# Moving the loads of twelve MoE weights on the load queue, with a planner's tables set anew

## The chip, the core and the metric

The program runs on one core of one Trainium2 chip. The core has a matrix engine (TensorE, PE in the rows; its weight loads are listed apart as PEld), three engines for elementwise work (VectorE: DVE, ScalarE: ACT, GpSimd: POOL), a queue engine (SyncE: SP) from which nearly all DMA transfers are issued, and 16 DMA engines. Each engine runs its own instructions in program order and waits on semaphores for the others. The metric is the device time of one execution in microseconds (us).

## What is computed

```python
def _attn_ref(q, k, v):                      # q, k, v: (4, 8, 576, 64)
    ...
    q_d = q.reshape(B, H, Sd, factor, D).mean(axis=3)
    ...
    out_d = sm_attn(q_d, k_d, v_d)
    out_up = np.repeat(out_d, factor, axis=2)
    pos = np.arange(S)
    mask = np.abs(pos[:, None] - pos[None, :]) < factor
    scores = scale * np.matmul(q, k.transpose(0, 1, 3, 2))
    scores = np.where(mask, scores, -1000000000.0)
    ...
    out_local = np.matmul(attn, v)
    return (out_up + out_local).astype(np.float32)
...
def _moe_ref(x, w1, w2, w3, w_out):          # (2304, 512) -> 768 -> 512
    h = np.maximum(np.maximum(x @ w1, x @ w2), x @ w3)
    return (h @ w_out).astype(np.float32)
...
def _moe2_ref(x, w_in, w_out):               # (2304, 512) -> 2048 -> 512
    h = x @ w_in
    g = np.maximum(0.01 * h, h)
    return (g @ w_out).astype(np.float32)
```

The attention's output goes through the first of these layers, and that one's through the second. `factor` is 4: one attention over tokens pooled by four, one over a band of seven tokens.

## The kernel before

The 2304 tokens are eight **units** of 288 tokens, two to a batch. A unit goes through attention, then through the first MoE layer on PE: 18 steps `L{u}.{x}` (line 900: 12 matmuls into `ps_h`, for one of six column blocks m and one of three weights e, x = 3m + e) and the second product `Y{u}.{o}` (line 932, `ps_o`). Every float32 product is made of three products of halves, so each weight tile has to be split first: ACT makes two pieces (lines 390 and 391), DVE joins them (two instructions), ACT or DVE copies the high half (line 377) and POOL subtracts for the low half (`wA<-wy,wA` or `wO<-wy,wO`, some 1.27 us). There are 24 such tiles of 512 KB: `wA{m}_{e}` (18) and `wO{m}` (6), numbered 0 to 23 in the list `W1`. When all units are through, a second phase (lines 1121 and 1165) does the second MoE layer; it takes the time from about 424 us to the end.

**The start, written out by hand.** The attention of unit 0 and the first eight weight splits follow the string `ORDER` (line 45), one word for one step. For head pair n of batch 0, `a`, `s` and `p` load the query and key tile `sqk`, the value windows `sv` and the pooled values `dsrawv`; `C D E H I O o P Q R S` are the local attention (C scores on PE, E the exponentials `ple` on ACT, O transposes, P times values, Q the sum `x`, R and S its halves `xh` and `xl`); `A B F G J K M m N v` with `L` are the attention over pooled tokens (L pools the values on POOL, N gives `ps_up`, v copies it to `up`). `w5` loads weight tile 5; `x5 y5 z5 u5` are the four steps of its split. `M3+11` means: 11 matmuls on a blank tile ahead of M3, to keep TensorE working.

**Twelve of the 24 weight tiles share memory with the start.** The `late` buffers hold `ple`, `dsqke`, `dsrawv`, `dsvaT` and `plt` of batch 0, and become the tiles of weights 12 to 23 (`wA4_0` to `wA5_2`, `wO0` to `wO5`). `load_after` names for each buffer the step that uses it last: N0 for weight 12, P0 for 13, M2 for 14, L3 for 15, P1 for 16, O2 for 17, then M3, N2, O3, P2, N3, P3. Right behind that word, `load_w1` (line 381) puts the weight's load on SP's queue, where it waits until the buffer is free; what stands behind it on SP waits too.

**Everything after the start** is ordered by `Plan.order`, a planner that runs while the program is built: it simulates five engines with written-down durations, and on each engine begins the ready step with the earliest due time. Due times come from the pace of the units (`LEN`, planned us of each unit), moved for each kind of step by `SHIFT`; `SLACK` and `FLOOR` say how long before its due time, and before which planned time, a step may not begin; `LOADED` is when the planner takes SP to be free of the start's loads. Kinds that matter here: `co` is the split of the `wO` tiles, `c` that of the `wA` tiles, `ds1` the pooled attention of batch 1, `@` the second phase. Where the planner sees PE stand, it puts matmuls on `ident` (line 884, `keep`) into the gap.

Of the kernel before, what the change touches and what calls it, by code (L numbers as in the profile page):

```python
# [62 lines left out]
CONV = 8  # L63
# [1 line left out]

SHIFT = {"@": 13, "pv": 28.7, "ra": 42.5, "t": -60.1, "mu": 41.9, "c": 22.4, "ds3": -74.5, "ds2": -60.8, "pl3": -11.7, "pl1": 24.8, "co": 13.8, "pl2": 1.2, "ds1": 0.7}
SLACK = {"ds1": 107.4, "pv": 71.4, "c": 20, "mu": 155.4, "ds3": 65.3, "co": 9.5}
LEN = (56.9, 80.6, 30.2, 57, 39.6, 55.8, 30, 54.8)  # L70
GAP = 1.04
LOADED = 11.0
FLOOR = {}
BANKS = {"B": "early", "M": "at", "N": "mm", "O": "at", "C": "early"}
BOOST = {"at": 36.8, "early": 10.6}

# [1 line left out]
def kind(n):  # L78
    if n[0] == "@":
        return "@"  # L80
    if n[0] == "c" and int(n[2:]) >= NS:
        return "co"
    if n[0] == "t" or n[0] == "c":
        return n[0]
    if n[:2] in ("mu", "pm", "ps", "s1", "s2", "mk", "PV"):
        return {"mu": "mu", "PV": "ds" + n[2]}.get(n[:2], "pv")
    if n[0] in "rae":
        return "pv" if n[0] == "e" else "ra"
    if n[1].isdigit():
        return "pl" + n[1] if n[0] in "CDEHIOPQRSo" else "ds" + n[1] if n[0] in "ABFGJKMmNv" else ""  # L90
    return ""


class Plan:
# [22 lines left out]
    def order(self, due, shift, slack, gap):  # L117
# [27 lines left out]
        for n in due:  # L145
            due[n] += shift.get(kind(n), 0)
        begin = {n: max(due[n] - slack.get(kind(n), 1e9), st[n]["begin"], FLOOR.get(kind(n), -1e9)) for n in due}
        end, free, doing = {}, dict(dict.fromkeys(self.ENGINES, 0.0), SP=LOADED), {}
        left = {n: len(x["deps"]) for n, x in st.items()}
# [98 lines left out]
def local_global_attention_moe_kernel(  # L248
# [26 lines left out]
    W1 = [("A", m, e) for m in range(M1) for e in range(3)] + [("O", m) for m in range(M1)]  # L275
    w1_tag = {t: "w" + t[0] + "_".join(map(str, t[1:])) for t in W1}
    nl = len(W1) // 2
# [6 lines left out]
    load_after = {last[n]: nl + i for i, n in enumerate(sorted(last, key=lambda n: steps_.index(last[n])))}  # L284
# [65 lines left out]
    def scratch(first, kind, name):  # L350
        if first == 0:
            tag = "l3" if name == "wl3" else "b"
            return PS["0"].tile([128, 512], F32, tag=tag, bufs=6 if tag == "b" else 1, name=name)
        if kind == "mm":
            return mm_bank(name)
        return PS[kind].tile([128, 512], F32, tag=kind, name=name)
# [9 lines left out]
    def fill(t):  # L366
        for _ in range(fills[0]):
            T.matmul(out=t, lhsT=warm[:, :128], rhs=warm, start=True, stop=True)
        fills[0] = 0
# [9 lines left out]
    def load_weight(src, pool, name):  # L379
        w = pool.tile([128, 1024], I32, tag=name, bufs=1, name=name)  # L380
        nc.sync.dma_start(out=w, in_=src.bitcast(I32))
        return w, pool, name
# [41 lines left out]
    def conv_step(t):  # L424
        if t not in conv:
            conv[t] = split_steps(wr.pop(t), sup, P, 4, lambda: scratch("0" not in PS, "mm", "wl3"))
        r = next(conv[t])
        if r and t[0] == "A":
            wA[t[1:]] = r
        elif r:  # L430
            wO[t[1]] = r
        return r
# [99 lines left out]
    def pl_load(what, b, h, u=None):  # L532
        us = (0, 1) if b == 0 else (u,)
        if what == "a":
            t = pools[b].tile([128, 2 * S + 6], F32, tag="sqk", bufs=2 if b else 4, name="sqk")
            nc.sync.dma_start(out=t, in_=qk[b, h])
            if u in (None, 2 * b):
                dst[b, h, "q"], dst[b, h, "k"] = halves(t)
            for x in us:
                pl[x, h, "q"], pl[x, h, "k"] = t[:, :S], t[:, S:]  # L540
        elif what == "s":
            n, first = (1, u % 2) if b else (2, 0)
            t = pools[b].tile([KP, n, NBLK, 128], F32, tag="sv", bufs=1 if b else 4, name="sv")
            nc.sync.dma_start(
                out=t.rearrange("p u n d -> p (u n d)"),
                in_=vW[b, h][:, first * NBLK * 128 : (first + n) * NBLK * 128],
            )
            for k, x in enumerate(us):
                pl[x, h, "v"] = t[:KB, k]
        else:  # L550
            t = late_tile([QP, 2, 2, FAC, D], "dsrawv")
            nc.sync.dma_start(out=t.rearrange("p c h f d -> p (c h f d)"), in_=vP[0, h])
            dst[0, h, "vr"] = t

    def pl_pool_v(h):
        raw = dst.pop((0, h, "vr"))[:QC]
        dst[0, h, "vaT"] = late_tile([QC, 256 + 8 * QC], "dsvaT")
        v32 = dst[0, h, "vaT"][:, :256].rearrange("p (c h d) -> p c h d", c=2, h=2)
        P.tensor_tensor(out=raw[:, :, :, 0:2], in0=raw[:, :, :, 0:2], in1=raw[:, :, :, 2:4], op=ALU.add)
        P.tensor_tensor(out=v32, in0=raw[:, :, :, 0], in1=raw[:, :, :, 1], op=ALU.add)  # L560
        dst[0, h, "v"] = v32
# [310 lines left out]
    def mm_bank(name):  # L872
        banks_taken[0] += 1
        return PS["mm"].tile([128, 512], F32, tag="mm", name=name)
# [339 lines left out]
    with tc.manual_schedule(engines={ET.SP, ET.PE, ET.DVE, ET.Activation, ET.Pool}):  # L1214
# [4 lines left out]
        }  # L1219
        fills[0] = FILL0  # L1220
        fill(scratch(0, "", "warm_ps"))
        for w in ORDER.split():
            n = int(w[1])
            copy_on[0] = "DVE" if "'" in w else "ACT"
            fills[0] = int(w.split("+")[1]) if "+" in w else 0
            if w[0] == "w":
                load_w1(W1[n])
                if n == CONV - 1:
                    for t in W1[CONV:nl]:
                        load_w1(t)  # L1230
            elif w[0] in "aps":
                pl_load(w[0], 0, n)
            elif w[0] in "xyzu":
                conv_step(W1[n])
            elif w[0] == "L":
                pl_pool_v(n)
            else:
                steps[w[0]](0, n)
            if w[:2] in load_after:
                load_w1(W1[load_after[w[:2]]])  # L1240
        copy_on[0] = "ACT"
        fills[0] = 0
        PS.pop("0").release()
# [23 lines left out]
        for n in range(CONV, len(W1)):  # L1267
            f = lambda t=W1[n]: conv_step(t)
            go(f"cx{n}", "ACT", 1.3, f, begin=max(0.0, LOADED + 2.0 - 1.3 * (len(W1) - n)))
            go(f"cy{n}", "DVE", 1.4, f, [f"cx{n}"])  # L1270
# [135 lines left out]
        for u in range(NU):  # L1406
            base = sum(LEN[:u])
            pace = (LEN[u] - 10) / NS
            for x in range(NS):
# [56 lines left out]
        go("open4", "SP", 0.0, open_p2b, [f"st{NU - 1}.{o}" for o in range(4)] + [f"cu{n}" for n in range(CONV, len(W1))])  # L1466
        base2 = sum(LEN)

# [139 lines left out]
        for c in range(len(sups)):  # L1608
            t = 0.16 + 0.54 * sups[c][1] / SB
# [28 lines left out]
        done = 0.0  # L1638
        for n in pn.order(due, SHIFT, SLACK, GAP):
            x = pn.steps[n]  # L1640
# [86 lines left out]
```

## Time and profile before

| | us |
|---|---|
| median of 3 runs (lowest, highest) | 792.58 (792.56, 792.84) |
| the profiled execution's own time | 790.48 |
| its span, first to last instruction | 788.7 |
| PE busy; PEld busy | 767.2; 732.7 |
| DVE, ACT, POOL busy | 590.1, 453.2, 234.4 |
| mean granted TensorE clock | 0.991 of full |

The profile's times count from the first instruction. "Busy" adds the time in which an engine executes something; a PE that is busy may still be slower than it could be. The granted clock is 1.00 at 2.4 GHz and 0.50 at 1.2 GHz. The profiled execution is 2.1 us below the median of the runs, and its own time 1.8 us above its span.

### The profile page before, as it was taken

How to read it: one execution, taken by the hardware profiler on the slowest of the kernel's cores; microseconds unless marked ns; L12 is line 12 of the kernel's file. 1: busy time of each engine (PE TensorE's matmuls, PEld its weight loads, DVE VectorE, ACT ScalarE, POOL GpSimd, SP SyncE). 2: the span in 40 equal slices, each digit the busy share in tenths (PEclk: the TensorE clock that was granted, in tenths of full speed). 3: DMA queues.
4: the chain of work that ended last, by engine and by line, in shares of the span. 5: the costliest groups of instructions: out<-in, count | busy, mean ns of one | idle time of the engine just before them, and what ended most of it. 6: DMA issues, size and time to landing. Idle time of an engine off the chain costs nothing.

```text
span 788.7 us, 16482 instructions
## 1 busy us (share of the span) xinstructions
PE 767.2 (97%) x6182; PEld 732.7 (93%) x6182; DVE 590.1 (75%) x1076; ACT 453.2 (57%) x1534; POOL 234.4 (30%) x221
## 2 busy tenths in 40 slices
PE   8799899999999999999999999999999999999997
PEld 4488789989999999999999999999999999999996
DVE  6678855777987887848687886666688898878681
ACT  7588738875358842225266886776778443333330
POOL 5678779787878653100000000000000000000000
PEclk9979999999999999999999999999999999999999
DMA  9891144364343121223334568675798645453522
GB/s 304 265 406 43 57 161 136 119 204 165 89 129 98 46 66 48 72 73 100 99 108 138 200 245 305 238 261 213 238 345 295 211 127 168 129 148 109 151 72 63
DMA packets 53519, 127.08 MB, mean 161 GB/s; under 512 B 4992, under 2 KB 18176, under 8 KB 53440
## 3 DMA queue, kind: packets, MB, share of 16 engines
q1 hardware_dynamic: 48640, 121.06, 46.2%
q10 hardware_dynamic: 4800, 4.98, 1.8%
q8 instruction: 48, 0.79, 0.4%
q14 instruction: 31, 0.25, 0.1%
HBM read 90.37 MB, written 35.65 MB: 160 GB/s over the span
## 4 chain that ended last, share of the span: by engine, by line
PE 71%; POOL 5%; DVE 2%; issue 2%; ACT 1%; DMA 1%; ACTq 0%; DVEq 0%; POOLq 0%
PE acc L1165 22%; PE ps_h L900 19%; PE ps_y L1121 12%; PE ps_o L932 7%; PE ps_z L1121 6%; PE ps_x L1121 3%; POOL qkprod L240 2%; POOL ple L240 1%; DMA gd<-g 1%; PE ps_up L791 1%; POOL hl L240 1%; PE ps_x L831 0%; POOL sqk L240 0%; PE ps_aT L770 0%; DVE pvprod L240 0%
## 5 line engine op out<-in xcount | busy, mean ns | idle before, releaser
L900 PE MATMUL ps_h<-xh,wA 128*128 128x288 f32 x1152 | 199.9, 301 | 2.1 <-DVE x L240 1.3
L1165 PE MATMUL acc<-w,gs 128*128 128x256 f32 x1512 | 178.0, 280 | 0.0
L1165 PEld LDWEIGHTS acc<-w,gs 128*128 128x128 f32 x1512 | 177.7, 189 | 0.2 <-DVE ob L240 0.2
L900 PEld LDWEIGHTS ps_h<-xh,wA 128*128 128x128 f32 x1152 | 167.1, 188 | 7.6 <-issue 4.5
L1148 ACT ACTIVATE gs<-gr 128x1792 fp32r<-128x1792 f32 x36 | 61.0, 1703 | 90.5 <-DVE gr L240 55.9
L1121 PE MATMUL ps_y<-xop,w 128*128 128x288 f32 x768 | 110.1, 295 | 1.5 <-ACT u L1090 0.9
L900 PE MATMUL ps_h<-xl,wA 128*128 128x288 f32 x576 | 109.0, 296 | 0.0
L1121 PEld LDWEIGHTS ps_y<-xop,w 128*128 128x128 f32 x768 | 104.4, 189 | 2.3 <-ACT u L1090 1.1
L900 PEld LDWEIGHTS ps_h<-xl,wA 128*128 128x128 f32 x576 | 88.0, 189 | 0.0
L240 DVE TENSOR_TENSOR gs<-gr,gs 128x1792 fp32r<-128x1792 f32 x36 | 72.7, 2022 | 12.6 <-ACT gs L1148 12.3
L932 PE MATMUL ps_o<-hh,wO 128*128 128x288 f32 x384 | 79.7, 301 | 0.0
L240 POOL TENSOR_TENSOR qkprod<-lq,lk 128x1344 f32<-128x1344 f32 x24 | 73.7, 3078 | 7.6 <-issue 2.4
L470 ACT ACTIVATE qkprod<-qkprod 128x64 f32<-128x64 f32 x280 | 67.3, 245 | 9.5 <-POOL qkprod L240 8.3
L240 DVE TENSOR_TENSOR gr<-gr 128x256 f32<-128x256 f32 (+1 forms) x108 | 54.2, 511 | 19.4 <-DMA gr<-gd 17.8
L240 DVE TENSOR_TENSOR hm<-hm,ps_h 128x288 f32<-128x288 f32 x96 | 43.1, 449 | 27.4 <-PE ps_h L900 26.8
L932 PEld LDWEIGHTS ps_o<-hh,wO 128*128 128x128 f32 x384 | 61.1, 188 | 2.1 <-issue 1.4
L932 PE MATMUL ps_o<-hl,wO 128*128 128x288 f32 x192 | 56.7, 295 | 0.0
L1121 PE MATMUL ps_z<-xop,w 128*128 128x288 f32 x384 | 56.0, 294 | 0.0
L470 ACT ACTIVATION_READ_ACCUMULATOR qkprod<-qkprod 128x1 f32 x280 | 53.4, 191 | 0.0
L1121 PEld LDWEIGHTS ps_z<-xop,w 128*128 128x128 f32 x384 | 52.6, 189 | 0.0
L1102 ACT ACTIVATE g<-g 128x288 f32<-128x288 f32 x96 | 41.4, 442 | 17.5 <-DVE g L240 17.0
L240 DVE TENSOR_TENSOR g<-u,ps_z 128x288 f32<-128x288 f32 x64 | 28.5, 452 | 25.6 <-PE ps_z L1121 19.4
(142 smaller groups left out, 1217.7 us busy)
## 6 DMA issues: line engine op xcount, KB each, us to landing
gd<-g SPq DMA_DIRECT2D x32, 576.0 KB, 4.4
gr<-gd SPq DMA_DIRECT2D x32, 512.0 KB, 4.1
sqk<-in_qk_dram SPq DMA_DIRECT2D x20, 579.0 KB, 4.1
wA<-in_wa_dram SPq DMA_DIRECT2D x18, 512.0 KB, 9.8
wl<-in_w_in_dram SPq DMA_DIRECT2D x16, 512.0 KB, 3.5
wl<-in_w_out_dram SPq DMA_DIRECT2D x16, 512.0 KB, 6.0
wd<-w2y SPq DMA_DIRECT2D x8, 896.0 KB, 4.6
w2y<-wd SPq DMA_DIRECT2D x8, 896.0 KB, 6.4
```

The lines of the kernel that those rows point to most:

```text
L240: self.last = f(*args, **kwargs)
L470: A.activation(out=pr[:, r, j], in_=pr[:, r, j], func=AF.Copy, accum_out=sc[:, r, j : j + 1])
L791: T.matmul(out=ps[64 * hh : 64 * hh + 64, :SD], lhsT=dst[b, h, "v"][:, kc, hh], rhs=dst[b, h, "aT", kc][:, 2 * hh : 2 * hh + 2].rearrange( ...
L900: T.matmul(out=ps, lhsT=wA[m, e][wi][:, kk * 128 : kk * 128 + 128], rhs=xx[:, kk] if u < PEU else xx[:, :, kk, :], start=n == 0, stop=n == ...
L932: T.matmul(out=ps, lhsT=wO[m][wi][:, os_], rhs=xx[:, m], start=m == n == 0, stop=m == M1 - 1 and n == 2)
L1102: A.activation(out=g, in_=g if src is None else blk.pop((q, src)), func=AF.Prelu, alpha=0.01)
L1121: T.matmul(out=ps, lhsT=w[:, kk * 128 : kk * 128 + 128], rhs=xx, start=j in (0, 1, 3) and n == 0, stop=n == 5, skip_group_check=True,)
L1148: A.activation(out=ga[i][:, 0], in_=gr[i], func=AF.Copy)
L1165: T.matmul(out=acc[c, j][:, k * 256 : k * 256 + 256], lhsT=a[:, m : m + 128], rhs=w, start=p == 0 and k == 0 and n == 0, stop=p == NP - 1 ...
```

## The change

Two things are edited. In the loop over `ORDER`, a load into a late buffer is no longer issued behind the buffer's last step but kept in a list `waiting`; once the word `w7` has come, the loads of weights 8 to 11 and all that was kept are issued in order of the weight, and from then on each further one behind its step as before. And the planner's tables have other values (two lines of them stand here).

```diff
-LEN = (56.9, 80.6, 30.2, 57, 39.6, 55.8, 30, 54.8)
+LEN = (56.8, 80.6, 38.5, 58.8, 37.8, 55.7, 30.9, 55)
 ...
-LOADED = 11.0
-FLOOR = {}
+LOADED = 7.0
+FLOOR = {"ds1": 15.6}
 ...
+        waiting, loaded = [], False
         for w in ORDER.split():
             ...
             if w[0] == "w":
                 load_w1(W1[n])
                 if n == CONV - 1:
-                    for t in W1[CONV:nl]:
-                        load_w1(t)
+                    loaded = True
+                    waiting[:0] = W1[CONV:nl]
 ...
             if w[:2] in load_after:
-                load_w1(W1[load_after[w[:2]]])
+                waiting.append(W1[load_after[w[:2]]])
+            while loaded and waiting:
+                load_w1(waiting.pop(0))
```

On SP's queue, this stood behind the value windows of head pairs 0 and 1 (`sv`, the first two rows), some 11 us into the program; `dsrawv_427`, `sv_429`, `sv_435` (head pairs 2 and 3) and the tiles `wA2_0`, `wA1_2`, `wA2_1` (weights 6, 5 and 7) belong to the start, the `wA4` and `wA5` tiles are late ones:

```order
L544 DMA sv_316<-in_vW_dram 112x768
L544 DMA sv_410<-in_vW_dram 112x768
L381 DMA wA4_0_417<-in_wa_dram 128x1024
L552 DMA dsrawv_427<-in_vP_dram 80x1024
L544 DMA sv_429<-in_vW_dram 112x768
L544 DMA sv_435<-in_vW_dram 112x768
L381 DMA wA4_1_444<-in_wa_dram 128x1024
L381 DMA wA2_0_447<-in_wa_dram 128x1024
L381 DMA wA4_2_471<-in_wa_dram 128x1024
L381 DMA wA1_2_500<-in_wa_dram 128x1024
L381 DMA wA5_0_510<-in_wa_dram 128x1024
L381 DMA wA5_1_527<-in_wa_dram 128x1024
```

And now, at the same place of SP's queue:

```order
L544 DMA sv_316<-in_vW_dram 112x768
L544 DMA sv_410<-in_vW_dram 112x768
L552 DMA dsrawv_425<-in_vP_dram 80x1024
L544 DMA sv_427<-in_vW_dram 112x768
L544 DMA sv_433<-in_vW_dram 112x768
L381 DMA wA2_0_443<-in_wa_dram 128x1024
L381 DMA wA1_2_494<-in_wa_dram 128x1024
L381 DMA wA2_1_529<-in_wa_dram 128x1024
L381 DMA wA2_2_531<-in_wa_dram 128x1024
L381 DMA wA3_0_533<-in_wa_dram 128x1024
L381 DMA wA3_1_535<-in_wa_dram 128x1024
L381 DMA wA3_2_537<-in_wa_dram 128x1024
```

The late tiles now follow behind `wA3_2`, in the order of their use; which loads there are and how many has not changed.

On POOL, in the planned part, the low halves of the last weights of unit 0 (`hl` is a low half of the unit's first layer, `xl` one of unit 1's input, `ple` a step of unit 1's attention) stood in this order:

```order
L240 TENSOR_TENSOR wO0_1072<-wy_998,wO0_1072 128x512
L240 TENSOR_TENSOR wO1_1078<-wy_1023,wO1_1078 128x512
L240 TENSOR_TENSOR hl_770<-hm_1049,hh_769 128x288
L240 TENSOR_TENSOR ple_1088<-ple_1088,plsm_1089 96x612
L240 TENSOR_TENSOR wO2_1188<-wy_1045,wO2_1188 128x512
L240 TENSOR_TENSOR xl_1115<-x32_1116,xh_1114 128x288
L240 TENSOR_TENSOR hl_770<-hm_1171,hh_769 128x288
L240 TENSOR_TENSOR wO3_1259<-wy_1128,wO3_1259 128x512
L240 TENSOR_TENSOR wO4_1261<-wy_1152,wO4_1261 128x512
L240 TENSOR_TENSOR wA5_0_1269<-wy_1209,wA5_0_1269 128x512
L240 TENSOR_TENSOR wA5_1_1296<-wy_1244,wA5_1_1296 128x512
```

and now in this one:

```order
L240 TENSOR_TENSOR wA5_0_1065<-wy_973,wA5_0_1065 128x512
L240 TENSOR_TENSOR dsrawv_1002<-dsrawv_1002 72x4x128
L240 TENSOR_TENSOR dsv32_1103<-dsrawv_1002 72x256
L240 TENSOR_TENSOR wA5_1_1099<-wy_1043,wA5_1_1099 128x512
L240 TENSOR_TENSOR wA5_2_1135<-wy_1080,wA5_2_1135 128x512
L240 TENSOR_TENSOR hl_770<-hm_1038,hh_769 128x288
L240 TENSOR_TENSOR ple_1165<-ple_1165,plsm_1166 96x612
L240 TENSOR_TENSOR wO0_1202<-wy_1106,wO0_1202 128x512
L240 TENSOR_TENSOR hl_770<-hm_1163,hh_769 128x288
L240 TENSOR_TENSOR wO1_1239<-wy_1138,wO1_1239 128x512
L240 TENSOR_TENSOR wO2_1256<-wy_1196,wO2_1256 128x512
L240 TENSOR_TENSOR wO3_1275<-wy_1219,wO3_1275 128x512
```

The three `wA5` tiles, which the last three steps of `L0` read, now come ahead of all `wO` tiles, which `Y0` reads after them; ACT and DVE have the same order of splits. The start's steps on PE, ACT, DVE and POOL stand in the same order as before.

## Rows read from the trace of the kernel before

**Rows 1.** Stretches: PE, PEld, DVE, ACT, POOL busy (instructions), clock, DMA share, GB/s.

```profile
0.00:46.70 46.70, 37.96 (x288) 22.37 (x288) 31.45 (x78) 31.71 (x116) 29.91 (x36) 0.89 0.90 306
46.70:100.00 53.30, 49.02 (x421) 44.92 (x420) 45.54 (x103) 40.70 (x124) 42.75 (x49) 0.97 0.39 140
100.00:420.00 320.00, 318.93 (x2586) 305.28 (x2585) 241.32 (x464) 171.46 (x908) 161.74 (x138) 1.00 0.33 106
420.00:605.00 185.00, 183.48 (x1383) 182.70 (x1382) 133.15 (x254) 140.59 (x330) 0.00 (x0) 1.00 0.70 253
```

**Rows 2.** Timeline of SP's queue: start, length, line, transfer, count.

```profile
11.10 2.72 SPq L544 DMA_DIRECT2D sv<-in_vW_dram  x2
25.23 0.35 SPq L381 DMA_DIRECT2D wA<-in_wa_dram  x1
...
27.10 13.05 SPq L381 DMA_DIRECT2D wA<-in_wa_dram  x12
```

**Rows 3.** Waits of SP's queue to 52 us: for whom, total, times, longest.

```profile
SPq L381 <- PE ps_up L791: 11.3, 1, 11.3
```

**Rows 4.** Transfers issued from 13.3 to 13.9 us: KB, us from issue to landing.

```profile
sv<-in_vW_dram SPq DMA_DIRECT2D x1, 336.0 KB, 11.2
```

**Rows 5.** Stretches of two us, columns as in rows 1.

```profile
24.00:26.00 2.00, 2.00 (x30) 1.49 (x28) 1.23 (x6) 0.93 (x2) 1.73 (x2) 1.00 0.02 6
...
34.00:36.00 2.00, 2.00 (x6) 0.73 (x5) 0.00 (x0) 0.00 (x0) 2.00 (x2) 0.50 1.03 412
36.00:38.00 2.00, 1.42 (x8) 0.60 (x6) 0.00 (x0) 0.62 (x2) 1.54 (x2) 0.86 1.02 414
...
48.00:50.00 2.00, 2.00 (x12) 1.58 (x11) 1.86 (x4) 2.00 (x4) 1.50 (x2) 0.50 1.03 420
```

**Rows 6.** Timeline of ACT: start, length, operation, [idle before <-who ended it].

```profile
29.84 0.68 ACT L377 ACTIVATE dsvaT<-ps_aT 72x288 f32<-72x288 f32 x2
37.38 0.66 ACT L390 ACTIVATE wy<-wA 128x512 f32<-128x512 f32 x1 [6.86 <-DMA wA<-in_wa_dram]
...
40.40 0.67 ACT L390 ACTIVATE wy<-wA 128x512 f32<-128x512 f32 x1
```

**Rows 7.** Timeline of POOL at the pooled values of head pair 3.

```profile
31.11 1.26 POOL L240 TENSOR_TENSOR dsrawv<-dsrawv 72x512 f32<-72x512 f32 x1 [3.31 <-DMA dsrawv<-in_vP_dram]
```

**Rows 8.** Timeline of PE from the blank matmuls ahead of M3 to the end of L0.0.

```profile
32.93 4.24 PE L368 MATMUL ps_aT<-warm 128*128 128x512 bf16 x11 [1.46 <-DVE up L240]
37.00 0.41 PE L770 MATMUL ps_aT<-ident,dsqke 72*72 72x72 f32 x4
39.60 0.44 PE L770 MATMUL ps_aT<-ident,dsqke 72*72 72x72 f32 x4 [2.18 <-ACT ple L607]
40.57 1.23 PE L791 MATMUL ps_up<-dsvaT 72*64 72x144 f32 x8 [0.53 <-ACT ple L607]
...
46.73 0.61 PE L900 MATMUL ps_h<-xh,wA 128*128 128x288 f32 x1
...
51.08 0.29 PE L900 MATMUL ps_h<-xh,wA 128*128 128x288 f32 x1
```

**Rows 9.** Timeline of PE in unit 0 where it stood, and its first ps_o.

```profile
68.06 0.73 PE L884 MATMUL ps_h<-ident 128*128 128x224 bf16 x6 [1.05 <-DVE hm L240]
...
83.15 0.93 PE L884 MATMUL ps_h<-ident 128*128 128x224 bf16 x8 [1.11 <-DVE hm L240]
...
88.00 0.37 PE L900 MATMUL ps_h<-xh,wA 128*128 128x288 f32 x1 [1.33 <-DVE x L240]
...
89.31 0.53 PE L900 MATMUL ps_h<-xh,wA 128*128 128x288 f32 x2 [0.80 <-POOL wA L240]
...
95.58 0.43 PE L932 MATMUL ps_o<-hh,wO 128*128 128x288 f32 x2
```

**Rows 10.** Timeline of POOL at the low halves of wO3 and wO4, then wA5_2.

```profile
85.51 2.50 POOL L240 TENSOR_TENSOR wO<-wy,wO 128x512 fp32r<-128x512 f32 x2 [1.06 <-DVE wA L240]
...
92.41 1.27 POOL L240 TENSOR_TENSOR wA<-wy,wA 128x512 fp32r<-128x512 f32 x1
```

More of the change, by code (lines that the diff above doesn't have):

```diff
@@ L63 @@
 CONV = 8
-SHIFT = {"@": 13, "pv": 28.7, "ra": 42.5, "t": -60.1, "mu": 41.9, "c": 22.4, "ds3": -74.5, "ds2": -60.8, "pl3": -11.7, "pl1": 24.8, "co": 13.8, "pl2": 1.2, "ds1": 0.7}
-SLACK = {"ds1": 107.4, "pv": 71.4, "c": 20, "mu": 155.4, "ds3": 65.3, "co": 9.5}
-LEN = (56.9, 80.6, 30.2, 57, 39.6, 55.8, 30, 54.8)
+SHIFT = {"@": 8.7, "pv": 21.7, "ra": 7.2, "t": -44.8, "mu": 41.9, "c": 21.4, "ds3": -74.5, "ds2": -60.8, "pl3": -14.9, "pl1": 24.8, "co": 28.7, "pl2": 1.2, "ds1": -5.6}
+SLACK = {"ds1": 107.4, "c": 20, "mu": 155.4, "ds3": 65.3, "co": -32.2, "t": 17}
+LEN = (56.8, 80.6, 38.5, 58.8, 37.8, 55.7, 30.9, 55)
 GAP = 1.04
-LOADED = 11.0
-FLOOR = {}
+LOADED = 7.0
+FLOOR = {"ds1": 15.6}
 BANKS = {"B": "early", "M": "at", "N": "mm", "O": "at", "C": "early"}
```

## The prediction

> **What bounds the kernel now.** I read the stretches first, to see where PE stands still. From 100 us to the second phase PE is busy for 318.93 of 320 us, and in the next 185 us for all but 1.52; before 100 us it is not: 8.7 us of the first 46.7 and 4.3 of the next 53.3 are idle [rows 1]. So an edit can gain ahead of 100 us only, and what is gained there reaches the end if PE stays as full as it is behind it. Second, SP's queue: two `sv` loads, the last issued at about 13.5 us, then nothing until 25.23, and then twelve weight loads in a row [rows 2]; one wait of 11.3 us for N0's `ps_up` is the cause [rows 3]. The last `sv` landed 11.2 us after its issue, at 24.7 [rows 4], so the DMA engines ran dry: share 0.02 from 24 to 26 us, against 1.02 and 414 GB/s once the queue went on [rows 5]. Third, who stood for it: ACT for 6.86 us, until 37.38, for the tile of weight 6, with the exponentials E3 queued behind it [rows 6], and POOL for 3.31 us for the pooled values [rows 7]. PE's row of the start shows the end of the chain: eleven blank matmuls, M3's first half at 37.00, its second half only at 39.60, since it needs the bank that E3 reads, and `L0.0` at 46.73 [rows 8].
>
> **The change, part by part.**
>
> *The loads.* SP no longer stands behind N0. Of the six loads that matter, three are small (320, 336, 336 KB), then come the 512 KB of weights 6, 5 and 7. The first reuses a buffer whose last reader, O0, comes well ahead of N0 on PE, and all go out while the DMA engines still have work to 24.7. The small ones and weight 6 are 1.54 MB: at 414 GB/s [rows 5] 3.7 us, at the 306 GB/s of the whole start [rows 1] 5.0. Weight 6 lands between 28.4 and 29.7, weights 5 and 7 within 3.5 us more. ACT is free for it at 29.84 + 0.68 = 30.52 [rows 6]: the wait of 6.86 us goes. The pooled values land near 26, and POOL needs them only after its step before, so that wait goes as well. The twelve late loads each move behind seven others. With 19 tiles of 524 kB and 1.0 MB of small loads after 24.7, at 414 GB/s, the last lands at 24.7 + 26.5 = 51 us; the `wO` tiles were still being split at 85 us [rows 10]. No new wait there: cost 0. If that cover were gone, each missing tile would cost ACT its 1.3 us of transfer.
>
> *The chain that takes the wait's place.* ACT does weight 6 and E3 from 30.5 to 33.5 (they took 37.38 to 40.40 [rows 6]). But PE now stands on its own: the eleven blank matmuls wait for `up` until 32.93 and take 4.24 us at half clock to 37.0, as before, since nothing ahead of them has moved. So of ACT's 6.86 us PE gets only the 2.18 in front of M3's second half and the 0.53 in front of N2: M3 ends at 37.8 instead of 40.04. From N2 to `L0.0` before took 40.57 to 46.73, 6.16 us, all at clock 0.50 [rows 5, 8]. At full clock it is half of that, 3.1, or 3.7 if I leave some room between small steps: `L0.0` begins at 37.8 + 3.7 = 41.5 instead of 46.73, **5.2 us** sooner. `L0.0` itself, with its keep-alive matmuls, took 4.5 us at that clock (46.73 to 51.2); at full clock 2.4: its end is at 43.9, **7.3 us** sooner. ACT, DVE and POOL follow the first figure, PE the second. Through unit 0 the four are about equally full (PE 49.0, DVE 45.5, POOL 42.8, ACT 40.7 of 53.3 us [rows 1]), so I take **6.0**. The bounds: 2.7 (the two waits only, clock as before) and 7.3.
>
> *The clock.* It fell to 0.50 after the idle ahead of 32.93, came back during the blank matmuls (0.86 in 36 to 38), and fell again after PE had stood from 37.4 to 39.6 [rows 5, 8]. That second idle goes away, and dense small matmuls at 1.00 are in the trace too (24 to 26 us, 30 of them, PE busy throughout [rows 5]); so I take full clock. The Trainium skill (TensorE: Matmul & The Clock Gate, "The HAM clock gate") says that the low clock is the default and that sustained activity releases it. By that alone the work that began at 40.57 should have brought the full clock back well before 50; the row of 48 to 50 has 2.00 of 2.00 busy and still 0.50. The row decides: being busy is not enough here, and the low clock stays a rival.
>
> *The order in unit 0.* Four stands in 53 us: 1.05, 1.11, 1.33 and 0.80 [rows 9]. The last two are in front of `wA5` steps: `wA5_2`'s low half ends at 93.7 on POOL, and the first `ps_o` follows at 95.58, although `wO4` was ready at 88.0 [rows 9, 10]. With `wA5` ahead of `wO`, those 2.13 us go. In their place PE may wait for `wO4` in front of `ps_o`: it is now the last of the chain, with a step of E ahead of its copy on ACT. That costs nothing if `wO4` takes the place in time that `wA5_2` had. Between a gain of 4.3 (all four stands) and a loss of 4.3 (as many new ones) I take a gain of **1.5**, near the two that have a cause in the order.
>
> *The other tables.* They reorder steps from 100 us on. There PE has 1.07 us of idle to win [rows 1]; a poorer order costs, by its nearest row, what unit 0's stands are worth, 4.3. I take 0, since in the new order PE has the same steps, and DVE (241 of 320 us), ACT and POOL have room. Steps of the second phase become due 4.3 us sooner; PE hides them, and its own order there is a chain that does not change: 0, at most the 1.52 us of idle. The added Python costs the chip nothing.
>
> **Sum:** 6.0 + 1.5 = 7.5 us. The profiled execution, 790.48, would be 783.0; the median of the runs stands 2.1 above it, so 792.58 - 7.5 = **785.1 us**.
>
> **Rivals.**
>
> *The clock stays low* through 50 us, as it did before. Then `L0.0` gains 2.7 us only, and with the order 4.2: **788.4**. For it: the busy stretch at 0.50. Against it: the second idle is gone.
>
> *More is won.* The blank matmuls run at full clock as well (2.1 us), `L0.0` ends 7.3 sooner for all engines, and all four stands go: 2.1 + 7.3 + 4.3 = 13.7, at most **779**. Against it: everything ahead of 32.93 is as before. The Trainium skill (Perfetto Trace Analysis, "Identifying the Most-Contended Engine") calls the share of weight loads the better measure of PE's headroom; by PEld, 100 to 420 us has 14.7 us left instead of 1.07. But a stretch of small matmuls with PE full shows PEld at 1.49 of 2.00 [rows 5]: much of that is their shape, so it only adds to this rival's chance.
>
> *Given back.* In units 1 to 3 the new order makes PE wait for attention steps of DVE or POOL, by 4 to 7 us: about **791.5**, no change to be told. For it: DVE is three quarters full there, and all tables moved at once. Against it: PE's 1.07 us.
>
> *Slower.* The `wO` splits become the bound of unit 0. Before, PE took from 51.2 to 95.58 us for the other 17 steps, 44.4 with 4.3 of stands; from 43.9 on it has them behind it near 84, and cannot begin a `ps_o` before `wO4`'s low half. If ACT, with E and `hh` steps between, brings `wO4` later than 95.6 us, the time of the first `ps_o` before [rows 9], all is lost, and each us beyond it is one lost: at 97.5 **794.5**. By the forecast the first `ps_o` stands at 95.6 - 7.5 = 88, so it decides from a delay of 7.5 us. Against it: those splits start sooner by the 6 us.
>
> **How the numbers follow.** Forecast 0.53, clock low 0.18, more won 0.11, given back 0.10, slower 0.08. The forecast and its own spread cover 782.5 to 787.5. To leave out no more than 2 in 10, the range takes in the low clock and most of what lies below: **780.5 to 789.5**. About 0.2%, 1.6 us, is what runs of this kernel can tell from no change. Faster by more: 0.53 + 0.18 + 0.11 and a little of "given back", 0.85; within it 0.07; slower 0.08.
>
> **What would show it.** SP's queue has no gap between 17 and 30 us, and the DMA share no hole near 25; ACT begins weight 6 near 30.5 and E3 near 31.6; M3's second half follows its first at once; `L0.0` begins near 41.5, at clock 1.00; the first `ps_o` stands near 88; PE from 100 to 420 idles by no more than 2 us. Wrong, if `L0.0` starts later than 44, or if the lead at 100 us is not the lead at the end.

## The result, and the profile after

The changed kernel takes **783.61 us** (median of four runs, 782.19 to 786.43) against 792.57 for the kernel before beside it: a ratio of 0.9896 over all the runs (the two medians alone make 0.9887), 95% interval 0.9862 to 0.9930. The forecast was 785.1, with a range of 780.5 to 789.5.

The profiled execution of the changed kernel is the longest of its four runs (786.43, span 784.6), that of the kernel before (790.48) is shorter than all the runs of it beside these, so these two traces differ by 4.1 us where the medians differ by 9.0. Two more profiles of the changed kernel were taken: e11_again below (own time 780.97, the second shortest of its six runs) and e1_again (785.80, the longest of its six); the median of all sixteen runs is 782.3. The first profile and that of e11 ("the second") are read here, and e1's stands beside them where it says something else. The span splits into six stages on PE: up to the first matmul of `L0.0`; from there to the first `ps_o` of unit 0; to unit 1's first `ps_h`; units 1 to 3 up to unit 3's first `ps_o`; up to unit 7's first `ps_o`; to the end.

| us | to `L0.0` | unit 0 | to unit 1 | units 1 to 3 | to unit 7 | rest | span |
|---|---|---|---|---|---|---|---|
| before | 46.7 | 48.9 | 15.3 | 138.3 | 165.9 | 373.6 | 788.7 |
| after, first profile | 41.2 | 43.5 | 15.7 | 144.5 | 166.6 | 373.1 | 784.6 |
| after, second profile (e11) | 38.8 | 43.2 | 15.7 | 141.8 | 166.4 | 373.3 | 779.2 |
| after, e1 | 40.5 | 44.0 | 15.7 | 143.3 | 166.2 | 374.1 | 784.0 |

The gain lies in the start (5.5 to 8.0 us) and in unit 0 (4.8 to 5.6); 3.5 to 6.2 us of it are lost again in units 1 to 3. The rows for that, beginning with the stretches of the first profile (columns as in [rows 1]):

```profile
0.00:46.70 46.70, 38.66 (x331) 24.27 (x332) 36.04 (x85) 35.23 (x123) 33.37 (x42) 1.00 0.99 328
46.70:100.00 53.30, 51.66 (x453) 47.50 (x452) 42.94 (x100) 39.38 (x119) 41.97 (x46) 1.00 0.31 104
100.00:420.00 320.00, 317.38 (x2543) 304.27 (x2542) 242.15 (x468) 170.06 (x908) 159.19 (x135) 0.99 0.35 110
```

PE's idle from 46.7 to 100 us is 1.64 instead of 4.28 us, the clock of the start is 1.00 instead of 0.89, and the DMA share of the start 0.99 instead of 0.90. From 100 to 420 us PE idles 2.62 us, where it had 1.07 [rows 1]. SP's queue has lost its hole (timeline as in [rows 2]):

```profile
11.78 2.79 SPq L544 DMA_DIRECT2D sv<-in_vW_dram  x2
17.31 0.31 SPq L552 DMA_DIRECT2D dsrawv<-in_vP_dram  x1
17.67 1.62 SPq L544 DMA_DIRECT2D sv<-in_vW_dram  x2
19.95 18.82 SPq L381 DMA_DIRECT2D wA<-in_wa_dram  x13
```

The thirteen `wA` loads now go out from 19.95 us on; in [rows 2] one went out at 25.23, behind the wait, and twelve from 27.10. In the stretch 24 to 26 us, empty before (0.02 [rows 5]), the DMA engines are full (but at 213 GB/s, half of what they move later), and two later stretches that stood at clock 0.86 and 0.50 are at 1.00:

```profile
24.00:26.00 2.00, 1.22 (x14) 0.71 (x14) 1.97 (x4) 0.51 (x1) 0.72 (x1) 1.00 1.05 213
36.00:38.00 2.00, 2.00 (x17) 1.21 (x17) 1.48 (x6) 2.00 (x8) 1.58 (x2) 1.00 1.04 414
48.00:50.00 2.00, 2.00 (x17) 2.00 (x17) 1.78 (x5) 2.00 (x7) 1.82 (x4) 1.00 1.04 424
```

ACT's wait of 6.86 us for weight 6 [rows 6] is 0.66 in the first profile, nothing in the second and 2.19 in e1 (one row of each, in this order):

```profile
33.55 0.67 ACT L390 ACTIVATE wy<-wA 128x512 f32<-128x512 f32 x1 [0.66 <-DMA wA<-in_wa_dram]
...
30.46 0.68 ACT L390 ACTIVATE wy<-wA 128x512 f32<-128x512 f32 x1
...
33.24 0.68 ACT L390 ACTIVATE wy<-wA 128x512 f32<-128x512 f32 x1 [2.19 <-DMA wA<-in_wa_dram]
```

PE in the start, first profile (columns as in [rows 8]):

```profile
34.91 2.55 PE L368 MATMUL ps_aT<-warm 128*128 128x512 bf16 x11 [1.50 <-DVE up L240]
37.30 0.67 PE L770 MATMUL ps_aT<-ident,dsqke 72*72 72x72 f32 x8
...
41.20 0.40 PE L900 MATMUL ps_h<-xh,wA 128*128 128x288 f32 x1
...
44.81 0.29 PE L900 MATMUL ps_h<-xh,wA 128*128 128x288 f32 x1
```

The eleven blank matmuls run at full clock, 2.55 us instead of 4.24 [rows 8]; M3's two halves follow each other without the 2.18 us between. This profile reached the blank matmuls 2.0 us later than the kernel before. Some 0.7 us of that stood already at 14 us, ahead of the first load that moved. The rest goes back to DVE, which stood 2.12 us, until 23.63, for a `sqk` load of the start: issued at 9.29 us, it took 14.3 us to land, against 11.9 in the kernel before (issued at 8.82). Whether the moved loads, which share the DMA engines with it from 17 us on, slowed it is not shown. The second profile does not have that lag:

```profile
32.46 2.55 PE L368 MATMUL ps_aT<-warm 128*128 128x512 bf16 x11 [0.94 <-DVE up L240]
34.85 0.67 PE L770 MATMUL ps_aT<-ident,dsqke 72*72 72x72 f32 x8
...
38.75 0.40 PE L900 MATMUL ps_h<-xh,wA 128*128 128x288 f32 x1
...
58.91 0.54 PE L884 MATMUL ps_h<-ident 128*128 128x224 bf16 x4 [0.71 <-DVE hm L240]
...
70.83 0.54 PE L884 MATMUL ps_h<-ident 128*128 128x224 bf16 x4 [0.88 <-DVE hm L240]
...
82.00 0.53 PE L932 MATMUL ps_o<-hh,wO 128*128 128x288 f32 x2
```

The rows at 58.91 and 70.83 are what is left of unit 0's stands: 0.71 and 0.88 us instead of 1.05, 1.11, 1.33 and 0.80 [rows 9]; the two in front of the `wA5` steps are gone, and the first `ps_o` is at 82.0 (84.65 in the first profile) instead of 95.58.

### The profile page after: what moved, and what is told of

It is laid out like the page before. It is cut to its first block, busy times and chain, and to the rows that moved or that the text cites. A ratio compares the mean times of both kernels' runs of the same rounds, so it can differ in the third digit from the quotient of the medians.

```text
span 784.6 us, 16494 instructions
## 1 busy us (share of the span) xinstructions
PE 765.3 (98%) x6186; PEld 732.6 (93%) x6186; DVE 590.8 (75%) x1078; ACT 453.3 (58%) x1532; POOL 234.5 (30%) x221
## 4 chain that ended last, share of the span: by engine, by line
PE 83%; POOL 5%; DVE 4%; DMA 4%; issue 2%; ACT 1%; ACTq 0%; DVEq 0%; SPq 0%; POOLq 0%
PE ps_h L900 25%; PE acc L1165 23%; PE ps_y L1121 13%; PE ps_o L932 8%; PE ps_z L1121 6%; PE ps_x L1121 3%; DMA sqk<-in_qk_dram 2%; POOL qkprod L240 2%; PE ps_sc L722 1%; DVE wl L240 1%; PE ps_up L791 1%; DMA dsrawv<-in_vP_dram 1%; DVE wy L240 1%; POOL wA L240 1%; PE ps_lo L652 1%
## 5 line engine op out<-in xcount | busy, mean ns | idle before, releaser
L900 PE MATMUL ps_h<-xh,wA 128*128 128x288 f32 x1152 | 200.5, 302 | 0.0
L900 PEld LDWEIGHTS ps_h<-xh,wA 128*128 128x128 f32 x1152 | 168.1, 190 | 5.2 <-issue 3.1
L900 PE MATMUL ps_h<-xl,wA 128*128 128x288 f32 x576 | 110.2, 298 | 0.4 <-POOL xl L240 0.2
L900 PEld LDWEIGHTS ps_h<-xl,wA 128*128 128x128 f32 x576 | 88.6, 190 | 1.1 <-POOL xl L240 1.1
L470 ACT ACTIVATION_READ_ACCUMULATOR qkprod<-qkprod 128x1 f32 x280 | 55.3, 198 | 0.0
```

The lines of the kernel that those rows point to most:

```text
L470: A.activation(out=pr[:, r, j], in_=pr[:, r, j], func=AF.Copy, accum_out=sc[:, r, j : j + 1])
L900: T.matmul(out=ps, lhsT=wA[m, e][wi][:, kk * 128 : kk * 128 + 128], rhs=xx[:, kk] if u < PEU else xx[:, :, kk, :], start=n == 0, stop=n == ...
```

## The experiments

All twelve stand here; "before" is the kernel before, run beside each on the same chip. A ratio is taken over all the runs and can differ a little from the quotient of the medians.

| | median, us (runs) | before | ratio, 95% interval |
|---|---|---|---|
| e1_again, changed kernel | 782.23 (6) | 792.38 | 0.9873, 0.9843 to 0.9902 |
| e2_loads_only | 783.63 (6) | 792.38 | 0.9890, 0.9864 to 0.9916 |
| e3_tables_only | 789.83 (12) | 792.38 | 0.9974, 0.9950 to 0.9999 |
| e4_keep_on | 782.49 (6) | 792.38 | 0.9870, 0.9845 to 0.9896 |
| e5_no_blanks | 784.75 (12) | 791.14 | 0.9935, 0.9908 to 0.9963 |
| e6_w6_late | 790.31 (12) | 791.14 | 0.9977, 0.9949 to 1.0006 |
| e7_wO_early | 790.87 (12) | 791.14 | 0.9985, 0.9960 to 1.0010 |
| e8_before_fill | 790.83 (12) | 791.86 | 0.9978, 0.9958 to 0.9997 |
| e9_fewer_blanks | 786.01 (6) | 791.86 | 0.9912, 0.9887 to 0.9937 |
| e10_w6_late_look | 788.94 (1) | 791.86 | |
| e11_again, changed kernel | 781.86 (6) | 790.95 | 0.9881, 0.9853 to 0.9909 |
| e12_loads_only | 785.50 (6) | 790.95 | 0.9925, 0.9897 to 0.9952 |

**The two parts apart.** The changed kernel again (e1, e11), the moved loads with the tables of before (e2, e12), and the new tables with the loads where they were (e3).

```diff
 e2, e12: the changed kernel with
+SHIFT, SLACK, LEN, LOADED, FLOOR of the kernel before
 e3: the changed kernel with
-        waiting, loaded = [], False
 ...
+                load_w1(W1[load_after[w[:2]]])
```

> The changed kernel once more. Its four runs lay between 782.19 and 786.43 us, those of before mostly within 0.3 us. Theory A (PE's clock falls in only some executions, near 207 us, where PE stood for 1.5 us in the profiled one): runs spread again over 4 us, median 782 to 785, and a profile whose clock does not fall there is 2 to 4 us shorter than the first. Theory B (the first profile is how it always runs): spread under 1 us, about 785.

> Only the loads are moved; the planner's tables are those of before. If the lead comes from the loads (my theory): L0.0 begins at 41 to 42 us, and the time is 785 to 787.5, since the stands in front of the wA5 steps (1.33 and 0.80 us) come back. If the tables carry it (rival): 789 to 793. The first ps_o should stand at 88.5 to 91.

> Only the tables are changed; the loads are issued as before. My theory: SP stands to 25 us as before and L0.0 begins at 46.5 to 47; the new order of the splits alone gives 1 to 3 us in unit 0, and the planner now expects the loads sooner than they come: 789 to 793. Rival (the tables carry the gain): 784 to 787.

> The changed kernel once more, beside the moved loads alone, to settle two things: whether its time is that of its second look (782.2) or nearer to that with 8 blank matmuls (786.0), and what the tables are worth on top of the loads. Theory A (the tables' lead of unit 0 is mostly given back in units 1 to 3): 782 to 784.5, and 0.5 to 2.5 us below the moved loads alone. Theory B (the lead is kept in most executions, the profiled ones fell into the low clock at the seam of units 2 and 3): 3 us or more below the moved loads alone.

> The moved loads with the planner's tables of before, once more, on the same chip as the changed kernel. Theory A (most of unit 0's lead given back): 784 to 786, 0.5 to 2.5 us above the changed kernel beside it. Theory B: 3 us or more above it.

The loads alone take 8.8 us off in the first set of runs and 5.4 in the second, the tables alone 2.6 (0.1 to 4.0 by the interval). Over both sets the changed kernel has a median of 782.0 us (12 runs) and the loads alone 784.6 (12 runs), so on top of the loads the tables are worth some 2.6 us as well (the means differ by 2.5, 95% interval 1 to 4): 1.4 in one set and 3.6 in the other. Neither theory of the last pair is shown outright; the two sets lie on either side of the line drawn between them.

The stages tell more. Moved loads with old tables: 38.8, 49.5, 15.3, 138.4, 165.9, 375.7 us (e2) and 40.2, 51.3, 15.3, 138.4, 165.9, 374.6 (e12). New tables with old loads: 45.5, 44.1, 15.7, 144.7, 166.1, 373.2 (e3). So the start follows the loads, and unit 0 and units 1 to 3 follow the tables.

Part of the difference in unit 0 is the clock. The old tables keep the stands in front of the `wA5` steps (1.33 and 0.81 us in e12), and in the profiles of e12, e2 and e8 (below) the clock fell at them, for some 7, 3 and 7 us, as it did not in the kernel before. In no profile with the new tables is there such a stretch in unit 0 behind 50 us. A row of e12, then one of e8:

```profile
84.00:88.00 4.00, 4.00 (x19) 3.96 (x18) 1.92 (x6) 2.13 (x7) 4.00 (x4) 0.50 0.00 0
...
88.00:92.00 4.00, 3.62 (x15) 3.62 (x16) 3.47 (x8) 3.59 (x13) 4.00 (x5) 0.50 0.00 0
```

Why unit 0 wins what units 1 to 3 lose shows in the attention's matmuls of unit 0, grouped by line (busy, mean ns of one, idle before); first with the old tables, e12:

```profile
L579 PE MATMUL ps_ls<-sqk 64*96 64x102 f32 x60 | 3.9, 260 | 0.0
L631 PE MATMUL ps_lt<-ident,ple 96*102 96x96 f32 x24 | 3.0, 267 | 0.0
...
L652 PE MATMUL ps_lo<-plt,sv 102*64 102x96 f32 x38 | 2.4, 254 | 0.0
```

and with the new ones, e11:

```profile
L579 PE MATMUL ps_ls<-sqk 64*96 64x102 f32 x48 | 3.1, 260 | 0.0
L631 PE MATMUL ps_lt<-ident,ple 96*102 96x96 f32 x18 | 2.0, 245 | 0.0
L652 PE MATMUL ps_lo<-plt,sv 102*64 102x96 f32 x26 | 1.7, 254 | 0.0
```

Twelve matmuls fewer of L579, six of L631 and twelve of L652 (and two of L571): one head pair of unit 1's local attention is no longer done in unit 0. In a timeline such a group takes 0.77, 0.70, 0.72 and 0.42 us, 2.6 together. In units 1 to 3 of the same two traces its L652 and L631 come back, with eight of L722 that stood ahead of unit 1 before, where its L579 and L571 are now:

```profile
L652 PE MATMUL ps_lo<-plt,sv 102*64 102x96 f32 x84 | 5.0, 254 | 0.0
...
L631 PE MATMUL ps_lt<-ident,ple 96*102 96x96 f32 x42 | 4.6, 245 | 0.0
...
L722 PE MATMUL ps_sc<-dsqk 64*72 64x144 f32 x40 | 3.6, 297 | 0.0
```

```profile
L652 PE MATMUL ps_lo<-plt,sv 102*64 102x96 f32 x96 | 5.7, 255 | 0.0
...
L631 PE MATMUL ps_lt<-ident,ple 96*102 96x96 f32 x48 | 5.3, 245 | 0.0
...
L722 PE MATMUL ps_sc<-dsqk 64*72 64x144 f32 x48 | 4.6, 298 | 1.0 <-ACT aT L377 1.0
```

(first e12, then e11). By these rows that is 0.7 + 0.7 + 1.0 = 2.4 us of work moved in, and the last row has a stand of 1.0 us on top. About half of unit 0's gain over the kernel before was work put off.

**The seam of units 2 and 3.** In the new order PE stands twice there, for ACT. In e11 nothing more came of it; in the first profile of the changed kernel the clock fell behind it (PE timeline of e11, then of the changed kernel):

```profile
203.91 0.44 PE L770 MATMUL ps_aT<-ident,dse 72*72 72x72 f32 x4 [0.54 <-ACT up L377]
205.35 1.01 PE L722 MATMUL ps_sc<-dsqk 64*72 64x144 f32 x8 [1.00 <-ACT aT L377]
206.28 0.79 PE L900 MATMUL ps_h<-xh,wA 128*128 128x288 f32 x4
```

```profile
206.50 0.44 PE L770 MATMUL ps_aT<-ident,dse 72*72 72x72 f32 x4 [0.54 <-ACT up L377]
207.94 1.53 PE L722 MATMUL ps_sc<-dsqk 64*72 64x144 f32 x8 [0.99 <-ACT aT L377]
209.40 1.33 PE L900 MATMUL ps_h<-xh,wA 128*128 128x288 f32 x4
```

The stands are equal to 0.01 us, yet in the second block eight L722 take 1.53 instead of 1.01 us and four L900 1.33 instead of 0.79. The stretch behind them, changed kernel (clock 0.50) and e11 (1.00):

```profile
208.00:212.00 4.00, 4.00 (x19) 3.63 (x20) 3.86 (x6) 0.18 (x1) 2.58 (x5) 0.50 0.33 107
```

```profile
208.00:212.00 4.00, 4.00 (x32) 4.00 (x32) 3.86 (x7) 1.96 (x9) 3.33 (x2) 1.00 0.48 148
```

This is the 2.7 us by which the two profiles differ in units 1 to 3 (144.5 and 141.8). In e1 the same stands were followed by some 3 us at 0.50, and units 1 to 3 took 143.3. Of the eight profiles with these stands (e3, e5, e6, e9 and e10 have them too) the clock fell in five and stayed at 1.00 in three (e6, e10, e11). The Trainium skill (TensorE: Matmul & The Clock Gate, "The HAM clock gate") says of the start of a kernel that how much work runs at the low clock differs from run to run. These traces show the same in the middle of one, behind stands of 1.5 us in all. Filling the seam was one experiment: the planner's matmuls on `ident`, allowed up to 150 us of the planned time, allowed up to 400, which adds 19 of them there.

```diff
-KEEP_TO = 150.0
+KEEP_TO = 400.0
```

> The changed kernel with the planner's fill-in matmuls allowed up to 400 us of planned time instead of 150: 19 more of them, all at the seam of units 2 and 3, where PE stood in the first profile and its clock fell to 0.50 for 7 us. Theory A (the low clock there costs 3 to 4 us): clock 1.00 from 205 to 216 us, unit 3 begins 2 to 4 us sooner against the same profile's first ps_o of unit 2, median 780.5 to 782.5 and a smaller spread. Rival: the 19 matmuls only take their 2 us, no change.

Its profile shows no stretch below 1.00 up to the last few us, and 142.2 us in units 1 to 3, but its median, 782.49, is not below the 782.23 of e1, nor is the median of its mean clocks (0.998) above that of e1 (0.999). Its profile alone cannot show that the matmuls kept the clock, since e6, e10 and e11 kept it without them; and if they did, it was worth less than these runs can tell.

**Weight 6.** In the changed kernel, the loads of weights 8 to 11 ahead of those of weights 6, 5 and 7: no gap on the queue, only other tiles first.

```diff
+                if n == 6:
+                    for t in W1[CONV:nl]:
+                        load_w1(t)
                 load_w1(W1[n])
                 if n == CONV - 1:
                     loaded = True
-                    waiting[:0] = W1[CONV:nl]
```

> The changed kernel with the loads of weights 8 to 11 put ahead of the load of weight 6: the same transfers without a gap on the queue, but weight 6 lands later by four tiles of 524 kB, 5.1 us at the 414 GB/s of the trace before. Theory A (the gain of the loads is the landing of weight 6, which holds ACT, the exponentials E3 and M3): ACT waits some 5 us for it, M3's second half stands 2 to 3 us behind its first, the clock falls to 0.50, L0.0 begins near 45 to 46, and the time is 4 to 6 us above the changed kernel: 786 to 788. Theory B (the gain is that the DMA engines no longer run dry, whichever tile comes first): the time is within 1.5 us of the changed kernel, 781 to 783.7.

> A second look at the kernel with the loads of weights 8 to 11 ahead of weight 6, whose profiled execution was one of its fast ones. Theory A (its slow runs are the clock): a run near 788 to 791 shows more than the 8 us at clock 0.50 of the first look, mean clock near 0.991. Theory B: as many us at 0.50 as in the first look, and longer waits of ACT for weight 6.

The order of those tiles costs 8.3 us against the changed kernel's 782.0 (7.9 by the ratios to the kernel before on each chip, 0.9977 and 0.9877), more than the 4 to 6 expected, and leaves 0.8 us of the gain, which these runs cannot tell from none. The three small loads go out early here as in the changed kernel, so they are not what won the time. Rows of e10, ACT and then PE:

```profile
36.68 0.66 ACT L390 ACTIVATE wy<-wA 128x512 f32<-128x512 f32 x1 [6.19 <-DMA wA<-in_wa_dram]
```

```profile
35.14 0.41 PE L770 MATMUL ps_aT<-ident,dsqke 72*72 72x72 f32 x4
38.90 0.69 PE L770 MATMUL ps_aT<-ident,dsqke 72*72 72x72 f32 x4 [3.35 <-ACT ple L607]
...
46.03 0.61 PE L900 MATMUL ps_h<-xh,wA 128*128 128x288 f32 x1
```

This is the start of the kernel before again, with full DMA engines: a wait of 6.19 us on ACT (6.86 in [rows 6]), M3 in two halves, and `L0.0` at 46.03 (46.73 in [rows 8]). Weights 5 and 7 came later too, but ACT goes on to them without a wait, at 39.71 and 43.33. In e6, whose profiled run (787.45, span 785.7) lies 2.9 us below its median, M3's halves were 1.42 us apart and `L0.0` began at 43.2. Theory B, that full DMA engines were the gain, falls. That the price is above 5.1 us is only partly explained: by its windows e10 ran some 10 us at clock 0.50 and e6 some 7, and the mean clocks of the twelve runs, median 0.9915, lie below those of both profiles (0.993 and 0.994), so that most runs had more of it.

**The clock of the start.** Two edits at the word M3 of the changed kernel, and one in the kernel before.

```diff
 e5: the changed kernel      e9: the changed kernel      e8: the kernel before
-M3+11                      -M3+11                      -M3+11
+M3+0                       +M3+8                       +M3+24
```

> The changed kernel without the eleven blank matmuls ahead of M3. Theory A (the clock is a term of its own in the gain: the blank matmuls now end at full clock, and M3 to L0.0 follow at full clock): PE stands some 3 us ahead of M3 (the exponentials E3 still end near 36.7 us), the granted clock falls to 0.50 as it did in the kernel before, the small steps from M3 to L0.0 take some 6 us instead of 3.5, L0.0 begins near 43.5 to 44.5 instead of 38.6 to 41.2, and the time is 2 to 3 us above the changed kernel: 784 to 785.5. Theory B (the clock decides nothing here, the chain of ACT and DVE sets the pace): L0.0 begins within 1 us of the changed kernel and the time is within 1 us of it, 781.5 to 783.

> The changed kernel with 8 blank matmuls ahead of M3 instead of 11. In the profile of the changed kernel the eleven end at 37.3 us, and E3 at 36.7, so the last three stand in M3's way. Theory A (eight are enough for the clock): M3 0.6 us sooner, the mean clock as in the changed kernel, the time 0 to 0.7 us below it. Theory B (the eleven hold the clock up): the mean clock of the runs falls below 0.995 and the time rises by 1 to 3 us, towards that without any blank matmul.

> The kernel before with 24 blank matmuls ahead of M3 instead of 11; the loads stay where they were. The blanks cover most of the stretch from 32.9 to 39.6 us in which PE stood for the exponentials E3, so the granted clock should come back during them and stay. Theory A (half of the gain of the change is the clock, which its moved loads keep up): M3's second half is still held by weight 6 and E3 near 39.6, but M3 to the end of L0.0 runs at 1.00; the mean clock of the runs rises from some 0.992 to 0.996 or more and the time falls by 3 to 5 us, to 787 to 789, against 792 for the kernel before on this chip. Theory B (the clock in the start is a companion, the chain of ACT decides): the time is within 1.5 us of the kernel before.

Without blank matmuls (e5) the clock falls and the time is 2.8 us above the changed kernel's 782.0 (4.6 by the ratios on each chip). PE's rows, and a stretch:

```profile
34.48 0.94 PE L770 MATMUL ps_aT<-ident,dsqke 72*72 72x72 f32 x8 [2.15 <-POOL dsqke L240]
...
41.64 0.61 PE L900 MATMUL ps_h<-xh,wA 128*128 128x288 f32 x1
```

```profile
36.00:40.00 4.00, 4.00 (x30) 2.83 (x30) 3.40 (x9) 4.00 (x9) 4.00 (x4) 0.50 1.02 414
```

From M3 to `L0.0` it is 7.16 us at the low clock; the changed kernel has 3.90 (37.30 to 41.20, and 34.85 to 38.75). That is as theory A had it, though `L0.0` began at 41.64, sooner than its 43.5 to 44.5; this profile (789.09, the second longest of the twelve) has the low clock at the seam as well. But e8 speaks against the wider reading that the clock by itself is half of the gain: the kernel before with 24 blank matmuls was expected at 787 to 789 and is at 790.83, 1.0 us below the kernel before (1.7 by the ratio, 0.2 to 3.3 by its interval). Its rows:

```profile
32.40 5.35 PE L368 MATMUL ps_aT<-warm 128*128 128x512 bf16 x24 [0.99 <-DVE up L240]
37.59 0.41 PE L770 MATMUL ps_aT<-ident,dsqke 72*72 72x72 f32 x4
39.19 0.44 PE L770 MATMUL ps_aT<-ident,dsqke 72*72 72x72 f32 x4 [1.18 <-ACT ple L607]
40.16 0.71 PE L791 MATMUL ps_up<-dsvaT 72*64 72x144 f32 x8 [0.53 <-ACT ple L607]
...
45.52 0.61 PE L900 MATMUL ps_h<-xh,wA 128*128 128x288 f32 x1
```

```profile
36.00:40.00 4.00, 2.45 (x17) 1.22 (x14) 1.39 (x2) 3.05 (x15) 1.01 (x1) 1.00 1.03 421
40.00:44.00 4.00, 3.37 (x34) 2.57 (x36) 3.65 (x10) 4.00 (x11) 3.33 (x4) 0.84 1.03 420
44.00:48.00 4.00, 4.00 (x29) 3.49 (x26) 3.01 (x6) 2.99 (x7) 3.89 (x4) 0.50 1.02 418
```

The 24 blanks run at full clock (5.35 us), but M3's second half still waits for E3, PE stands 1.18 and 0.53 us, and the clock falls behind that, from 42 us on. This profile is not the common case: it is the second longest of the twelve runs (792.78, mean clock 0.991, as low as any), and its clock fell once more in unit 0, behind the stands for `wA5` (the row of 88 to 92 above; its unit 0 took 51.6 us). The median mean clock of the runs rose from 0.991 to 0.995. The five runs with 0.996 and more, in which the clock can have been low for some 7 us in all (an estimate: twice 0.004 of 790 us, rounded up), took 788.8 to 791.8 us: with the clock up nearly throughout, most of the gain is still missing. M3's second half, which waits for ACT, began at 39.19 in the profile and at 39.60 in [rows 8].

With eight blanks (e9) neither theory holds as written: `L0.0` of its profile began at 40.8 and unit 7's first `ps_o` at 409.9, as in e1, and yet the median is 786.01, 3.8 us above e1 (2.8 above e1 and e11 by the ratios, as theory B had it). The mean clock, 0.996, is lower than in e1 (0.999) and e11 (0.9975), but not below the 0.995 of theory B. It ran on another chip than these, and its six runs spread over 5.4 us; this one is left open.

**The order of the splits.** The two values for `co` as before, in the changed kernel.

```diff
-SHIFT "co": 28.7    SLACK "co": -32.2
+SHIFT "co": 13.8    SLACK "co": 9.5
```

> The changed kernel with the two values for the kind co (the splits of the wO tiles) as they were before; the planner then puts five wO splits ahead of the last two wA5 splits again and rearranges much around them. Theory A (wA5 ahead of wO is what brings the first ps_o forward, and the rest of the tables gives part of it back): PE stands 2 us or more ahead of the last wA5 steps, the first ps_o comes at 87 us or later, measured from an L0.0 at 41, and the time is at or above that of the moved loads with the old tables, 783.6 to 786. Theory B (the order of the splits is worth nothing to the end, since units 1 to 3 give it back in any case): the time is within 1 us of the changed kernel, 781.3 to 783.2.

The time is 790.87, far above the 783.6 to 786 that theory A started from, at a mean clock (median 0.997) that does not explain it. Unit 0 takes 50.2 us instead of 43.2, as theory A has it, but PE also stands 2.43 us for `hl` at 204 and 1.39 for `xh` at 258, so the price is not that of the splits alone: with the other numbers left, the planner builds another order throughout. The run shows that the numbers hang together, and does not price the splits.

## Why the prediction was right, point by point

**The loads.** Right in mechanism: the hole on SP is gone, most of the wait of 6.86 us with it, and e6 and e10 show that weight 6 was the tile that mattered. But its landing was put too early, between 28.4 and 29.7 us, from rates of 306 and 414 GB/s. From 20 to 28 us, with the moved loads under way, the DMA engines were full and moved 237 to 257 GB/s in the first profile. Weight 6 took 13.5 us from its issue at 19.95 and landed at 33.5. In the nine profiles with the loads moved and weight 6 ahead of weights 8 to 11 it landed between 27.9 and 33.5, and only in three (e2, e4, e11) did ACT find it ready, at 30.35 to 30.46 (the prediction had 30.52); in the other six ACT waited 0.45 to 2.37 us for it. `L0.0` goes with it: in the eight of them that keep the blank matmuls, the order in which ACT begins weight 6 (30.35 to 33.55) is the order in which `L0.0` begins (38.6 to 41.2). So part of the wait was still there in six of the nine.

**The chain that takes its place.** From M3 to `L0.0` took 3.90 us in the first and the second profile; the forecast's 37.0 to 41.5 is 4.5. `L0.0` began at 41.2, 40.5 (e1) and 38.75 (e11), forecast 41.5. The step that was wrong is the blank matmuls: taken at half clock "as before, since nothing ahead of them has moved", they ran at full clock, 2.55 instead of 4.24 us. That is no work of the change: with the loads where they were, in e3 and e8, they ran at full clock too (2.55 for them in e3), so the 4.24 in [rows 8] should not have been carried over from one execution. With M3 held by E3 it changed little: e3's `L0.0` began at 45.5. With the loads moved it is the 1.7 us (2.1 there) of the "more is won" rival. That the first profile still comes near 41.5 is luck: the blanks were 1.7 us shorter and were reached 2.0 us later. In the other direction, `L0.0` itself took 3.7 to 4.3 us and not 2.4, because its second half now comes at the pace of `xl` from POOL (a stand of 0.61 us for it in e1, 0.23 in the first profile). The term, 6.0, measured 5.5 to 8.0 in the profiles and 5.4 to 8.8 by the runs of the loads alone.

**The clock.** Taken at 1.00, and it was, against the rival with 788.4: in none of the eight profiles with weight 6 sooner and the blank matmuls kept is there a low clock ahead of 80 us. What e8 adds is that the clock is worth little without the load: in its profile the clock fell again behind M3's second wait, and its runs with the highest mean clocks were hardly faster than the kernel before.

**The order in unit 0.** The two stands with a cause in the order went, as forecast, and a bit of the other two: 1.59 us are left of 4.29. The forecast's 1.5 against 2.6 by the runs (tables alone, or on top of the loads, all tables together) is a fair size. But the view on which it was to be judged, the first `ps_o`, showed 82.0 to 84.7 instead of 88: one head pair of attention, 2.6 us, had been put off, and the lead there was partly borrowed.

**The other tables.** The step that failed. They were put at 0 "since in the new order PE has the same steps"; PE has them over the whole, not in each stage. Units 1 to 3 take 3.5 us longer, 2.4 for moved work and 0.8 for stands (1.9 for 1.1), and 5.0 (e1) or 6.2 (first profile) where the clock falls at the seam. PE's idle from 100 to 420 us is 2.62 and 4.01 (e11) where at most 2 was allowed. And by the prediction's own test, the lead ahead of 100 us (10.5 at unit 1's first `ps_h`) is not the lead at the end (4.1; 13.2 and 9.5 in the second profile), so that sign says "wrong" while the time came out right: the sum of 7.5 held because the start and unit 0 together gave more than their terms and the units behind gave back what unit 0 had borrowed. The mechanism of the loads was right; that the sum fits as well as it does is in part luck, errors of opposite sign.

**The spread.** The prediction took 0.2%, 1.6 us, for what runs can tell apart, from three runs within 0.3 us. The kernel before spread over 6 to 10 us in each set of 11 to 29 runs beside the experiments, and the interval of the result is 0.34% to either side.

**Rivals.** "Slower" did not come: the first `ps_o` waits for no `wO4`. "Given back" is there in its place (units 1 to 3, ACT rather than DVE or POOL), but with some 1 us of stands in every profile of the changed kernel and 1.5 (e1) or 2.7 more in those in which the clock falls, not 4 to 7.

## What to carry to other kernels

A load whose buffer comes free late belongs behind the loads that can go at once; a queue that waits holds all that stands behind it, and the price is set by the one tile that a busy engine needs next (here four tiles in its way cost 8.3 us). And loads that go out together may land later than their bytes at the best rate say: here 2 to 4 us later in six of nine profiles. When a planner's tables change, count the steps of each stage before and after, by line and shape: a lead at a stage boundary may be work put off. And a gap of a TensorE that waits for another engine is worth closing at its cause; filling it with blank matmuls (e8) raised the mean clock by 0.004 and won some 1 of 9 us.

## What the runs showed of the hardware

Equal stands (0.54 and 1.00 us, 0.4 us of matmuls between them) took the clock to 0.50 in five profiles and not in three others; where it fell in the changed kernel, it cost 1.5 (e1) and 2.7 us (first profile). A TensorE busy for 4.00 of 4.00 us stood at 0.50 there, as it did for 2.00 of 2.00 in [rows 5]. DMA engines that were full all the time moved 237 to 257 GB/s from 20 to 28 us in the first profile and 416 from 32 to 36. The executions of one kernel on one chip spread by 3 to 10 us in 790. Over the 29 runs of the kernel before beside e5 to e7 each 0.001 of mean clock went with 0.8 us (786.88 us at 0.999, 796.53 at 0.987), over the other three sets with 0.55 to 0.7. Whether that is a price is not shown: 0.001 of 790 us is 0.8 us, which would fit, but in e8 the mean clock rose by 0.004 and the time fell by 1.0 us, or 0.2 to 3.3 by the interval, where 0.8 for each 0.001 would make 3.2.
